# Gated linear attention with a mixture of experts on one core: written order for indirect writes, grouped logits, scan seeds in PSUM, a moved k-v product and early-expert tiles in the first stage's pools

## The chip, the cores and the metric

The kernel runs on 1 core of one Trainium2 chip. A core has TensorE (PE in the profile; PEld is its weight loading), VectorE (DVE), ScalarE (ACT), GpSimd (POOL) and SyncE (SP, which here only issues transfers), each with its own in-order queue of instructions, and 16 DMA engines. The metric is the time of one execution in microseconds on the device. The kernel before has been timed three times; the median is 460.03 us (457.02 to 463.07).

## The reference

First a gated linear attention over 4 batches, 8 heads, 768 tokens and a head dimension of 48, with a 48 x 48 state per head:

```python
for t in range(S):
    state = alpha[:, :, t, :, None] * state + np.einsum('bhd,bhe->bhde', k[:, :, t], v[:, :, t])
    y[:, :, t] = np.einsum('bhd,bhde->bhe', q[:, :, t], state)
```

Its output, 3072 tokens of 384 values, goes through a mixture of 8 experts (384 to 1024 to 384). A token takes the expert with its largest logit, unless a local gate says that it stays with the expert of the token before it:

```python
logits = np.einsum('bsd,de->bse', x, w_gate)
local_gate = 1.0 / (1.0 + np.exp(-np.einsum('bsd,de->bse', x, w_local).squeeze(-1)))
...
        fresh_e = int(np.argmax(logits[b, s]))
        if s == 0 or local_gate[b, s] < 0.5:
            e = fresh_e
        else:
            e = prev_e if prev_e >= 0 else fresh_e
        ...
        h = np.maximum(x[b, s] @ w1[e], 0.0)
        out[b, s] = p[e] * (h @ w2[e])
```

All values are fp32.

## The kernel before, in words

**Attention, 24 blocks.** A block is 128 tokens of one batch, cut into two chunks of 64; the four batches take turns, so block i + 4 continues block i. Four transfers bring `a` (the decays), `k`, `q` and `vt`. Two scans on VectorE, `scan1` forward and `scan2` backward, make products of decays; their second operand is a tile of seeds (`z1`, `z2`), and GpSimd multiplies `q` and `k` with the results in place. `mids` is a small fill by GpSimd of columns of `a`, which `scan1` of that block needs. TensorE then transposes `k` (`kt`, tile kp), multiplies k with q (`pm`, tile pe), k with v (`um`, tile up), and at last forms the output (`ym`, tile y); VectorE masks pe (`mask`), adds the k-v products to the state (`sums`) and carries the state on (`carry`); ScalarE copies states (`first`, tile sb) and results out of PSUM. The block's rows XR go to DRAM (xd), are transposed (`xt`, tile xp), copied to xx, and multiplied with the gate weights (`logit`, tile lg).

The loop at `for i in range(NB + 2)` is a software pipeline over these steps: in pass i, `um`, `sums` and `ym` are those of block i - 1, the scans those of block i + 1, `kt` and `pm` those of block i, and `xt` and `logit` those of block i - 2. Three times in a pass `other()` advances all routing generators by one step each and runs the deferred VectorE work. Four blocks make a column of logits; `logits` and `route` turn columns into an expert number, a probability and a place in that expert's list, for spans of 2, 1, 2 and 1 columns. Each span ends with indirect writes by GpSimd (`ls<-pl,ix` in the profile): one for each block, 8, 4, 8 and 4 of them. In each pass TensorE also does dummy matmuls on the zero tile dz (DN of them, and DN0 = 48 at the start).

**The early expert.** Expert 0's weights come in during the attention stage and are split into a high and a low part (`Weights.split`), and each product is made of three matmuls. Its first 240 tokens (job a) are multiplied in the passes after the last block, its next 240 (job b) after them. `fast` finds job b's tokens for the last span by matmuls without waiting for the list to land.

**The ranked experts.** The other seven are sorted by their token count. For each there is a job with up to four tiles of 128 tokens or fewer: load the list (`li`), gather the tokens (`xg`, an indirect read), transpose and split (`tp`, `xh`, `xl`), first product (`h`, into `hh`, `hl`), second product (`yp`, `yo`), and an indirect write to `out`. The weights of the next expert are loaded and split between the slices of the current one (`piece`): the split's high part on ScalarE, its low part on VectorE or, for one piece (tile w1l), on GpSimd. At last a rarely taken loop treats tokens beyond a list's planned size, whose number is counted in `nt`, `ovt` and `cum`.

**Pools.** Attention's SBUF tiles are in the pool ap, its PSUM tiles in pp (tags kp, up, pe, y, xp, lg, rt; pe takes two banks, so all eight are taken). The early expert's tiles for job a are in m1 and pp. At the end of the `with` block both pools are given up, and the pools mp and qp take their memory; job b's products use mp and qp.

**Order.** A planner orders each engine's instructions by its own estimate of time, except where `keep_in_program_order` holds them to the order of the program; from the first block on that is asked for everything that goes through the `Engine` wrapper (line 80, hence "L80" in every row). `apart` declares that an indirect write does not depend on the earlier ones of its kind:

```python
for p in those:
    tc.declare_no_dep(w.ins, p, reason="every token has a place of its own")
those.append(w.ins)
```

## Time and profile before

| | |
|---|---|
| median of 3 runs | 460.03 us (457.02 to 463.07) |
| the profiled execution, its own time | 461.34 us |
| its span, first to last instruction | 459.5 us |
| mean granted TensorE clock | 0.956 |
| busy: PE, PEld, DVE, ACT, POOL | 416.8, 375.8, 258.7, 167.4, 173.3 us |
| moved by DMA | 64.79 MB |

The profile is one execution. Busy times are shares of the span; a busy TensorE isn't one at its peak, since its matmuls overlap and their ends are modelled. The granted clock is given as a share of full speed. "idle before" names what a waiting engine waited for, inferred from semaphores; "issue" means that nothing visible was waited for. In a row of a timeline the numbers are start and length in us, and brackets hold the idle time before it. In the chain of waits each piece is released by the one before it. The last instruction of TensorE ends at 450.8 us.

### The profile page before, as it was taken

The page shows a single profiled execution, that of the slowest core. Times are in us where ns is not written, and L with a number is a line of the kernel's source. Part 1 is how long each engine was busy: PE and PEld are TensorE (multiplying, and loading weights), DVE is VectorE, ACT ScalarE, POOL GpSimd, SP SyncE. Part 2 cuts the span into 40 slices and gives each one's busy share as a digit, 9 for nine tenths or more (in the row PEclk, how much of TensorE's full clock was granted, in tenths as well). Part 3 has the DMA queues.
Part 4 walks back from the last instruction along what each step waited for, and adds up shares of the span by engine and source line. Part 5 has one row for each costly group of instructions (what it writes and reads, how often), then busy time and mean ns, then how long its engine had stood idle before and what let it go on. Part 6 is the DMA issues. An engine that isn't in the chain of part 4 may idle for free.

```text
span 459.5 us, 10789 instructions
## 1 busy us (share of the span) xinstructions
PE 416.8 (91%) x4245; PEld 375.8 (82%) x4245; DVE 258.7 (56%) x436; ACT 167.4 (36%) x366; POOL 173.3 (38%) x233
## 2 busy tenths in 40 slices
PE   7699999949979988882999799999999999999992
PEld 7578878837858877772988698999999999999992
DVE  4878888927966852361455524634446536466420
ACT  1145555423543452200445314414415324363300
POOL 8433334384365512433525023333334114251012
PEclk9799999996998999996899899999999999999997
DMA  8889878784785610123457513533544716445001
GB/s 218 190 242 270 220 219 243 208 174 89 180 155 161 185 60 19 20 52 123 115 178 184 165 47 108 168 108 106 169 121 134 221 37 201 159 129 184 34 11 31
DMA packets 35476, 64.79 MB, mean 141 GB/s; under 512 B 9942, under 2 KB 17879, under 8 KB 35423
## 3 DMA queue, kind: packets, MB, share of 16 engines
q1 hardware_dynamic: 27420, 53.63, 42.1%
q0 software_dynamic: 6272, 10.09, 7.8%
q8 instruction: 34, 0.56, 0.6%
q10 hardware_dynamic: 1730, 0.36, 0.4%
q14 instruction: 20, 0.16, 0.2%
HBM read 54.51 MB, written 10.11 MB: 141 GB/s over the span
## 4 chain that ended last, share of the span: by engine, by line
PE 49%; issue 9%; POOL 5%; DVE 3%; DMA 2%; ACT 1%; POOLq 0%; SPq 0%; ACTq 0%
PE h_r L80 18%; PE yp_r L80 18%; PE y L80 3%; PE lg L80 2%; POOL out L80 2%; PE tp_r L80 1%; PE hp L80 1%; DMA ls<-pl,ix 1%; PE up L80 1%; POOL w1l_r L80 1%; PE yp_a L80 1%; POOL xg_r L80 1%; DMA rw_r<-w 1%; PE yp_b L80 1%; POOL ls L80 1%
## 5 line engine op out<-in xcount | busy, mean ns | idle before, releaser
L80 POOL DMA_INDIRECT out<-yo_r,li_r x25 | 27.2, 1089 | 116.5 <-DVE yo_r L80 112.6
L80 PE MATMUL yp_r<-w2h_r,hh_r 128*128 128x384 f32 (+4 forms) x200 | 69.7, 348 | 0.0
L80 PE MATMUL yp_r<-w2h_r,hl_r 128*128 128x384 f32 (+4 forms) x200 | 68.0, 340 | 0.0
L80 PE MATMUL yp_r<-w2l_r,hh_r 128*128 128x384 f32 (+4 forms) x200 | 67.9, 339 | 0.0
L80 PE MATMUL h_r<-xl_r,w1h_r 128*128 128x384 f32 (+5 forms) x168 | 59.9, 357 | 0.0
L80 PE MATMUL h_r<-xh_r,w1h_r 128*128 128x384 f32 (+5 forms) x168 | 59.8, 356 | 0.0
L80 PE MATMUL h_r<-xh_r,w1l_r 128*128 128x384 f32 (+5 forms) x168 | 59.7, 355 | 0.0
L80 DVE SCALAR_TENSOR_TENSOR hl_r<-h_r,hh_r 128x384 fp32r<-128x384 f32 (+5 forms) x56 | 33.3, 597 | 43.1 <-ACT hh_r L80 42.5
L80 ACT ACTIVATE hh_r<-h_r 128x384 fp32r<-128x384 f32 (+5 forms) x56 | 29.4, 525 | 66.4 <-PE h_r L80 66.2
L80 POOL TENSOR_TENSOR k<-k,sf 112x512 f32<-112x512 f32 x24 | 28.6, 1193 | 46.3 <-issue 39.5
L80 POOL DMA_INDIRECT xg_r<-xd,li_r x25 | 28.7, 1148 | 38.7 <-DMA li_r<-ls 28.9
L80 DVE TENSOR_TENSOR_SCAN A<-a,z 112x520 f32<-112x520 f32 x24 | 29.6, 1232 | 20.1 <-POOL a L80 20.1
L80 POOL TENSOR_TENSOR q<-q,A 112x512 f32<-112x512 f32 x24 | 28.4, 1183 | 31.3 <-DVE A L80 26.1
L80 PEld LDWEIGHTS yp_r<-w2h_r,hh_r 128*128 128x128 f32 (+4 forms) x200 | 36.7, 183 | 0.3
L80 PEld LDWEIGHTS yp_r<-w2l_r,hh_r 128*128 128x128 f32 (+4 forms) x200 | 36.6, 183 | 0.3
L80 PEld LDWEIGHTS yp_r<-w2h_r,hl_r 128*128 128x128 f32 (+4 forms) x200 | 36.5, 183 | 0.3
L80 DVE TENSOR_TENSOR w2l_r<-rw_r,w2h_r 128x768 fp32r<-128x768 f32 x28 | 34.5, 1232 | 2.9 <-ACT w2h_r L80 1.2
L80 DVE TENSOR_TENSOR_SCAN sf<-a,z 112x520 f32<-112x520 f32 x24 | 34.7, 1445 | 0.1
L80 PE MATMUL y<-sb,q 112*64 112x96 f32 x384 | 29.6, 264 | 4.3 <-ACT sb L80 4.1
L80 PEld LDWEIGHTS h_r<-xl_r,w1h_r 128*128 128x128 f32 x168 | 31.6, 188 | 2.2 <-DVE xl_r L80 0.3
L80 PEld LDWEIGHTS h_r<-xh_r,w1l_r 128*128 128x128 f32 x168 | 31.6, 188 | 2.0
L80 PEld LDWEIGHTS h_r<-xh_r,w1h_r 128*128 128x128 f32 x168 | 31.5, 188 | 2.0
(190 smaller groups left out, 793.7 us busy)
## 6 DMA issues: line engine op xcount, KB each, us to landing
rw_r<-w SPq DMA_DIRECT2D x21, 512.0 KB, 3.9
rw_r<-w SPq DMA_DIRECT2D x28, 384.0 KB, 3.5
a<-akq SPq DMA_DIRECT2D x24, 227.9 KB, 5.2
k<-akq SPq DMA_DIRECT2D x24, 224.0 KB, 4.2
q<-akq SPq DMA_DIRECT2D x24, 224.0 KB, 4.3
vt<-vn SPq DMA_DIRECT2D x24, 192.0 KB, 3.8
xd<-XR SPq DMA_DIRECT2D x24, 192.0 KB, 2.8
vt<-vn SPq DMA_DIRECT2D x24, 96.0 KB, 4.2
```

Of the source, the lines that this page charges most:

```text
L80: r = f(*a, **k)
```

## The change

- `order` adds, for each engine, an edge from every instruction to the one written before it. It is called in the wrapper and, for indirect writes, again in `apart`, after the declarations.
- `DN` falls from 4 to 2, and the dummies move from `logit` to the end of `pm`, into unused columns of pe.
- `logit` does nothing for three blocks and then the matmuls of four blocks, with the gate weights' slice as the outer loop; the blocks write partitions 0, 32, 64 and 96 of a tile in tag rt. The copy lc follows at once, and `logits` has one step less. xx is one tile for four blocks.
- The tag lg goes. Its bank holds `zp`, and `z1` becomes its first 260 columns; `scan1` runs in two halves of 260 over the same seeds.
- `um(i)` moves from the start of the next pass to the end of the pass, ahead of the last `other()`; `sums` and `first(i - 1, 1)` move to the start of the pass, ahead of `scan1(i + 1)`.
- `fast` runs the deferred work first.
- Job b keeps the pools m1 and pp, with job a's tags (xp, up, y, pe and kp); pp is given up only after job b, and the first ranked job transposes its tokens into xp.
- The overflow count's VectorE part moves into the first product of the first ranked job, its matmuls into the fourth slice of the second product.

```diff
-DN = 4
+DN = 2
...
-    pinned = [False]
+    pinned, behind, before = [False], {}, {}
+
+    def order(r):
+        e = r.ins.engine
+        p = behind.get(e)
+        if p == r.ins.name:
+            p = before[e]
+        if p is not None:
+            tc.add_manual_dep(r.ins, p, mybir.DependencyInfo(
+                mybir.DependencyClass.NoSync, mybir.DependencyReason.DATA), reason="written order")
+        behind[e], before[e] = r.ins.name, p
...
-                return tc.keep_in_program_order(r) if pinned[0] else r
+                if pinned[0]:
+                    tc.keep_in_program_order(r)
+                    order(r)
+                return r
...
             tc.declare_no_dep(w.ins, p, reason="every token has a place of its own")
+        order(w)
         those.append(w.ins)
...
-        z1 = ap.tile([R, SW], F32, bufs=1, name="z1")
+        HW = SW // 2
+        zp = pp.tile([128, 512], F32, tag="z", name="zp")
+        z1 = zp[0:R, 0:HW]
...
-            v_.tensor_tensor_scan(A, d["a"][:, 0:SW], z1, 0.0, ALU.mult, ALU.add)
+            for h in range(2):
+                w = slice(h * HW, (h + 1) * HW)
+                v_.tensor_tensor_scan(A[:, w], d["a"][:, w], z1, 0.0, ALU.mult, ALU.add)
...
+            for _ in range(DN):
+                t_.matmul(pe[:, 1, 256:496], lhsT=dz[:, 0:128], rhs=dz[:, 0:240], start=True, stop=True)
             d["pe"] = pe
...
         def logit(i):
-            c, o = i // G, i % G
-            xx = blk[i]["xx"]
-            if o == 0:
-                st["lg"] = pp.tile([128, 368], F32, tag="lg", name=f"lg_{c}")
-            lg = st["lg"]
+            c = i // G
+            if i % G < G - 1:
+                return
+            xx = st["xx"]
+            lg = pp.tile([128, 128], F32, tag="rt", name=f"lg_{c}")
             for k in range(3):
-                t_.matmul(lg[32 * o:32 * (o + 1), 0:128], lhsT=wgs[:, k, :], rhs=xx[:, k, :], start=(k == 0), stop=(k == 2))
-            for _ in range(DN if i + 2 < NB else 0):
-                t_.matmul(lg[:, 128:368], lhsT=dz[:, 0:128], rhs=dz[:, 0:240], start=True, stop=True)
...
+                for b in range(G):
+                    t_.matmul(lg[32 * b:32 * (b + 1), :], lhsT=wgs[:, k, :], rhs=xx[:, b, k, :],
+                              start=(k == 0), stop=(k == 2))
+            lc = ap.tile([128, 128], F32, tag="lc", bufs=1, name=f"lc_{c}")
+            s_.copy(lc, lg)
+            steps.append(logits(c, lc))
...
-            lp = [pp.tile([P, 3], F32, tag=t, name=f"lp_{t}") for t in ("rt", "lg")[0:ns]]
+            lp = [pp.tile([P, 3], F32, tag=t, name=f"lp_{t}") for t in ("rt", "kp")[0:ns]]
...
-        jb = Job("b", PART2, FIRST * RS + C1, m1, None, 2, 2, 9, 4, ("tp", 2), (("yp",), 3))
+        jb = Job("b", PART2, FIRST * RS + C1, m1, pp, 2, 1, 8, 2, ("xp", 1), (("up", "y"), 1))
...
             if 0 < i <= NB:
-                um(i - 1)
+                sums(i - 1)
+                first(i - 1, 1)
             if i + 1 < NB:
                 scan1(i + 1)
             if i < NB:
                 state0(i)
                 kt(i)
-            if 0 < i <= NB:
-                sums(i - 1)
-                first(i - 1, 1)
-            if i < NB:
                 pm(i)
...
             if i > 1:
                 logit(i - 2)
+            if i < NB:
+                um(i)
             other()
...
-    for j in jobs:
-        j.sp, j.ps = mp, qp
+    for j in jobs[1:]:
+        j.sp, j.ps = mp, pp
+    jobs[1].tpt = ("xp", 1)
...
+            if n == 1 and f == 4:
+                nt = mp.tile([8, 1], F32, bufs=1, name="nt")
+                gr = mp.tile([8, NOV], F32, bufs=1, name="gr")
+                v_.tensor_tensor(gr, cntp.broadcast_to([8, NOV]), cc("jt", 0, 8), ALU.is_gt)
+                v_.tensor_reduce(nt, gr, AX.X, ALU.add)
...
         for q, _ in enumerate(j.gemm2(W)):
+            if n == 1 and q == 3:
+                tp = qp.tile([8, 2], F32, tag="tp", name="ovt")
+                t_.matmul(tp[:, 0:1], lhsT=cc("tri8", 0, 8), rhs=nt, start=True, stop=True)
...
+        if n == 0:
+            pc.close()
+            qp = ctx.enter_context(tc.tile_pool(name="qp", bufs=2, space=PSUM))
+            for m in jobs[1:]:
+                m.ps, m.tpt = qp, ("tp", 2)
```

More of the change, by code (lines that the diff above doesn't have):

```diff
@@ L241, in store @@
                 bounds_check=NTOK - 1, oob_is_err=False))
-    with ExitStack() as ac:
+    ac, pc = ExitStack(), ExitStack()
+    pp = pc.enter_context(tc.tile_pool(name="pp", bufs=1, space=PSUM))
+    with ac:
         ap = ac.enter_context(tc.tile_pool(name="ap", bufs=2))
-        pp = ac.enter_context(tc.tile_pool(name="pp", bufs=1, space=PSUM))
         BW = HP * 128
         SW = 2 * HP * (C + 1)
-        z1 = ap.tile([R, SW], F32, bufs=1, name="z1")
+        HW = SW // 2
+        zp = pp.tile([128, 512], F32, tag="z", name="zp")
+        z1 = zp[0:R, 0:HW]
         z2 = ap.tile([128, SW], F32, bufs=1, name="z2")
@@ L805, in gla_moe @@
                     piece(Wn, (f - 3) // 2)
-        if n == 1:
-            nt = mp.tile([8, 1], F32, bufs=1, name="nt")
-            gr = mp.tile([8, NOV], F32, bufs=1, name="gr")
-            v_.tensor_tensor(gr, cntp.broadcast_to([8, NOV]), cc("jt", 0, 8), ALU.is_gt)
-            v_.tensor_reduce(nt, gr, AX.X, ALU.add)
-            tp = qp.tile([8, 2], F32, tag="tp", name="ovt")
-            t_.matmul(tp[:, 0:1], lhsT=cc("tri8", 0, 8), rhs=nt, start=True, stop=True)
-            t_.matmul(tp[:, 1:2], lhsT=cc("ones", 0, 8)[:, 0:8], rhs=nt, start=True, stop=True)
-            cum = mp.tile([8, 2], F32, bufs=1, name="cum")
-            v_.tensor_copy(cum, tp)
-            ti = mp.tile([8, 1], I32, bufs=1, name="ti")
-            v_.tensor_copy(ti, cum[:, 1:2])
         at_ = spread(nx.ns, 4 * j.ns) if nx else []
@@ L820, in gla_moe @@
         for q, _ in enumerate(j.gemm2(W)):
+            if n == 1 and q == 3:
+                tp = qp.tile([8, 2], F32, tag="tp", name="ovt")
+                t_.matmul(tp[:, 0:1], lhsT=cc("tri8", 0, 8), rhs=nt, start=True, stop=True)
+                t_.matmul(tp[:, 1:2], lhsT=cc("ones", 0, 8)[:, 0:8], rhs=nt, start=True, stop=True)
+                cum = mp.tile([8, 2], F32, bufs=1, name="cum")
+                v_.tensor_copy(cum, tp)
+                ti = mp.tile([8, 1], I32, bufs=1, name="ti")
+                v_.tensor_copy(ti, cum[:, 1:2])
             if nx and q in (0, 2):
```

36 lines of the change are left out of this document (17 added, 19 removed).

## The prediction

> **What bounds the kernel now.** I read the table by stretches first, with the stretches cut where TensorE changes its behaviour. The first row is one line of the answer on the tile XR, the copy that ends each block's attention.
>
> ```profile
> L80 ACT COPY XR<-y x24: 478/478/479, 21.0 to 182.8; 128x384 f32<-128x384 f32 x24
> ...
> 26.80:95.90 69.10, 68.04 (x1256) 55.24 (x1255) 58.62 (x92) 36.95 (x98) 28.25 (x37) 1.00 0.83 235
> 95.90:111.10 15.20, 9.10 (x115) 7.42 (x116) 6.66 (x14) 3.22 (x10) 9.73 (x13) 0.69 0.58 100
> 111.10:182.80 71.70, 66.26 (x1140) 53.92 (x1140) 47.08 (x89) 32.76 (x92) 30.02 (x35) 0.97 0.52 129
> ...
> 205.60:216.30 10.70, 1.23 (x9) 0.85 (x9) 1.86 (x8) 0.82 (x2) 4.81 (x5) 0.75 0.49 155
> 216.30:237.40 21.10, 20.71 (x133) 19.86 (x133) 10.71 (x19) 8.86 (x17) 7.52 (x6) 0.88 0.49 142
> ...
> 254.30:257.10 2.80, 0.04 (x1) 0.01 (x1) 1.90 (x4) 2.72 (x4) 0.00 (x0) 1.00 0.38 152
> 257.10:262.10 5.00, 4.98 (x23) 4.97 (x24) 2.59 (x4) 0.49 (x1) 0.00 (x0) 0.66 0.72 181
> 262.10:450.80 188.70, 188.70 (x1078) 183.88 (x1076) 91.67 (x125) 64.58 (x106) 56.99 (x46) 1.00 0.39 120
> 450.80:459.50 8.70, 0.00 (x1) 0.00 (x0) 0.62 (x1) 0.00 (x0) 1.32 (x1) 0.64 0.15 34
> ```
>
> The columns are the stretch and its length, busy time of PE, PEld, DVE, ACT and POOL, the granted clock, the DMA share and GB/s. Three kinds of stretch stand out. In 262 to 451 us TensorE is busy all of the time at clock 1.00, and the change leaves that work alone, as it does the 8.70 us behind it. In the attention stage (24 copies of XR from 21.0 to 182.8, so 23 block periods in 161.8 us, 7.03 us each) it is nearly always busy, except in 95.9 to 111.1. And there are two holes: 205.6 to 216.3 (1.23 of 10.70 us busy) and 254.3 to 257.1 (0.04 of 2.80). After each hole the clock is low for a while (0.88 and 0.66 over the next stretch), so a hole costs more than its length.
>
> One undisturbed block, from the chain of waits (start, length, what), and inside it the logits from the timeline of PE:
>
> ```profile
> 151.01 2.21 PE y L80 x48
> 153.22 1.42 PE lg L80 x10
> 154.63 0.81 PE up L80 x16
> 155.44 0.53 PE kp L80 x4
> 155.98 0.62 PE pe L80 x32
> 156.60 0.48 PE xp L80 x3
> ```
> ```profile
> 153.15 0.84 PE L80 MATMUL lg<-xx,wgs 128*32 128x128 f32 x6
> 153.92 0.71 PE L80 MATMUL lg<-dz 128*128 128x240 f32 x4
> 154.56 0.88 PE L80 MATMUL up<-vt,kk 128*48 128x96 f32 x16
> ```
>
> A block is 2.21 + 1.42 + 0.81 + 0.53 + 0.62 + 0.48 = 6.07 us of PE with nothing idle in between. 23 of them would be 139.6 us, so 22.2 us of the 161.8 are excess.
>
> **The change part by part.**
>
> *Written order for indirect writes.* This is what the planner made of group 0's eight list writes on POOL (first and last of eight), and what DVE and POOL did next:
>
> ```profile
> 91.28 1.43 POOL L80 DMA_INDIRECT ls<-pl,ix  x1 [1.50 <-DVE st L80]
> ...
> 100.86 0.98 POOL L80 DMA_INDIRECT ls<-pl,ix  x1 [0.30 <-issue]
> 101.85 1.19 POOL L80 TENSOR_TENSOR q<-q,A 112x512 f32<-112x512 f32 x1
> ...
> 105.61 1.18 POOL L80 TENSOR_TENSOR q<-q,A 112x512 f32<-112x512 f32 x1 [1.41 <-DVE A L80]
> 108.02 1.18 POOL L80 TENSOR_TENSOR k<-k,sf 112x512 f32<-112x512 f32 x1 [1.23 <-issue]
> ```
> ```profile
> 104.24 1.24 DVE L80 TENSOR_TENSOR_SCAN A<-a,z 112x520 f32<-112x520 f32 x1 [8.97 <-POOL a L80]
> 105.51 0.18 DVE L80 RECIPROCAL z<-A 112x4 f32<-112x4 f32 x1
> 105.61 0.53 DVE L80 TENSOR_TENSOR st<-up,st 112x384 f32<-112x384 f32 x1
> 106.05 1.83 DVE L80 TENSOR_TENSOR_SCAN sf<-a,z 112x520 f32<-112x520 f32 x1
> ```
>
> All eight stand in a row in front of one block's q product, so POOL gives nothing to the blocks for 10.6 us and the scan waits 8.97 us. The 15.20 us stretch holds one block: 15.2 - 6.07 = 9.1 us lost, partly as low clock (0.69). In written order at most two writes fall in one pass of the block loop, one after the k product and one after the small fill of "a" that the next scan needs. A write is (100.86 + 0.98 - 91.28) / 8 = 1.32 us on POOL. The one ahead of the fill makes the next scan late, the one behind it runs beside that scan. Group 0 and 1 have 12 writes and the early expert 2 gathers, 7 passes. I charge 1.0 us each, 7 us (bounds 0, where TensorE is the limit, and 7 x 1.32 = 9).
>
> *Dummies and logits.* Four dummies go from 153.92 to 154.56, 0.64 us; two stand in their place behind pe, 0.32 to 0.42 with the same edges, I take 0.40. The six real logit instructions take 0.77 us (153.15 to 153.92), 0.13 each, one behind the other. In the new form 24 stand together and neighbours write different column groups. Rows of this kind: up, two groups, 0.81 / 16 = 0.05 each at 96 columns, 0.067 at 128; pe, four quadrants, 0.62 / 32 = 0.02 at 64 columns. So 24 cost 0.9 us (four abreast, as pe) to 1.6 (two, as up) to 3.1 (no overlap), per block 0.23, 0.40, 0.77. I take 0.30; no gain below pe's price is in sight. PE per block becomes 6.07 - 1.42 + 0.40 + 0.30 = 5.35 us.
>
> *k-v product at the block's end, state sum ahead of the scan.* On PE "um" only changes places with its neighbours. On DVE it adds a wait: the state sum of block i-1, which needs that product, now stands ahead of scan 1 of block i+1, and behind it queue the scan, POOL's q, scan 2, POOL's k, and PE's transposes of k. From the rows above: scan at 104.24 to the end of k at 108.02 + 1.18 = 109.20 is 4.96 us, with the second scan stretched from 1.23 to 1.83 because q still runs on POOL. With the sum in front: 0.53 + 4.96 = 5.49 us from the end of one um to the start of the k transposes two blocks on. The PE work of that block follows, 5.35 us, and ends with its um. So two periods take at least 5.49 + 5.35.
>
> *Scan seeds in PSUM, in two halves.* The elements stay the same, one instruction more. A small DVE instruction is 0.18 us (the reciprocal), so between 0 and 0.36 is added; I take 0.15, since two instructions overlap at their edges as 105.51 and 105.61 do. Two periods: 5.49 + 0.15 + 5.35 = 11.0, a period of 5.5 us. That is above the 5.35 of PE: the loop over DVE and POOL becomes the limit by a little.
>
> ```profile
> L80 DVE TENSOR_TENSOR_SCAN A<-a,z x24: 1222/1228/1242, 4.7 to 158.8; 112x520 f32<-112x520 f32 x24
> ...
> 66.45 1.21 DVE L80 TENSOR_TENSOR w1l_a<-rw_a,w1h_a 128x1024 fp32r<-128x1024 f32 x1
> ```
>
> The minimum, median and maximum of the scan are the same, so nothing on POOL ever held it up, and moving its seeds buys nothing against today's neighbours. It matters for the write that will run beside it: the scan's wait for such a write would be up to 0.98 us in 7 passes, 3.5 us over pairs of passes, which my sum leaves out. The Trainium skill, "SBUF — State Buffer", section "SBUF: two separate sides", says that DVE with two SBUF inputs and GpSimd take one port pair in turns for a whole instruction; the stretched sf row agrees, and by that rule the scan with a PSUM operand is free of the lock, so leaving the 3.5 us out is right.
>
> In 13 blocks the early expert's weight splits (7 pieces, every second pass) stand between the two scans: 1.21 us for the row shown. Beside q they aren't free, I add 1.0: two periods 12.0, so 6.0 us. The attention stage: 13 x 6.0 + 10 x 5.5 = 133, + 7 for writes, + 5 (estimate: of today's 71.7 - 10 x 6.07 = 11 us of excess in 111.1 to 182.8 about half is routing work and the early expert's matmuls, which stay) = 145 us against 161.8. **Gain 17.**
>
> *One step less in the routing.* The logits' copy is no longer a step of its own; at the end each step is a slice of the early expert's matmuls, about 1 us. **Gain 1.**
>
> *Early expert on own buffers.* The hole, and what follows it up to the first ranked expert:
>
> ```profile
> 207.52 0.81 PE L80 MATMUL tp_b<-cs,xg_b 120*128 120x120 f32 x6 [0.35 <-PE ct L80]
> 216.26 0.54 PE L80 MATMUL h_b<-xh_b,w1h_a 128*128 128x240 f32 x1 [7.93 <-ACT xh_b L80]
> ...
> 215.34 0.82 ACT L80 CAST xh_b<-tp_b 128x360 fp32r<-128x360 f32 x2 [18.95 <-DMA out<-yo_a,li_a]
> ```
> ```profile
> 215.24 1.79 DMA li_r<-ls
> ...
> 220.62 1.00 POOL xg_r L80
> ...
> 224.51 2.41 POOL w1l_r L80
> 226.94 3.57 DMA rw_r<-w
> 230.54 1.06 ACT w1h_r L80
> ...
> 237.40 16.96 PE h_r L80 x72
> ```
>
> The cast has its input at 208.3 and waits until 215.3, for DMAs that have nothing to do with it: its tile lies in memory of a pool that must first be given up. With tiles of job a's pools that wait goes. One transposed tile at a time (one buffer) costs two rounds of transposes 0.4, cast 0.4 and difference 0.5: matmuls at about 210.0 instead of 216.26. Part b and the first transposes take 21.10 us at clock 0.88; at 1.00 that is 18.6, so PE could end at 228.6 instead of 237.4. What is late next: the list load ends at 217.0, three gathers at 1.3 each (ahead of the weight difference on POOL) bring 221.9, the difference 2.41, the load into its buffer 3.57, the cast 1.06: 229.0, and one more cast and difference until about 231. PE starts at 228.6 but waits inside its first group, as if it began at 230.7. **Gain 6.7** (9 if those weights come in time, 4 if the pool that is now given up between part b and the first ranked expert costs a wait).
>
> *Overflow count earlier.*
>
> ```profile
> 257.12 0.23 PE L80 MATMUL ovt<-nt,cs 8*8 8x1 f32 x4 [2.77 <-DVE nt L80]
> ```
>
> The count moves to the fourth slice, its matmuls into the second product: 2.77 us go, and 5.0 x (1 - 0.66) = 1.7 of low clock behind it. **Gain 4** of the 4.5, as some of it may meet weights that come no earlier.
>
> **Sum.** 17 + 1 + 6.7 + 4 = 29 against the profiled execution's 461.3 (span 459.5): 433. That execution is 1.3 us above the median of the runs, so **432 us**.
>
> **The rivals.** *TensorE stays the limit.* The new DVE wait is hidden and writes cost nothing: 23 x 5.35 + 5 = 128, a gain of 34, with the full 9 and 4.5: 417 us. For it: PE is the limit in every undisturbed block today. Against: the loop above is 5.5.
>
> *The loop keeps its old pace.* DVE is busy 58.62 of 69.10 us and the DMA share is 0.83 in 26.8 to 95.9. If that holds blocks at 6.07 us: 139.6 + 7 + 5 = 152, a gain of 10, and 4 + 3 elsewhere: 443 us.
>
> *The order does not spread the writes.* Then the 9.1 us stay and the 7 are saved, with a shorter burst of group 1 adding some 5: about 439.
>
> *The clock falls (slower).* Half the dummies go, and PE gets short pauses. In the row 257.1 to 262.1 a pause of 2.77 us was enough for 0.66. A block at half clock costs about 5 us more (5.35 doubled, less what overlaps); the gain of 29 is gone with 6 such blocks, and with 12 the time is 432 + 60 = 490. Against it: 111.1 to 182.8 has PE busy for 92% and a clock of 0.97, and my blocks of 6.0 us have PE busy for 89%. The Trainium skill, "TensorE: Matmul & The Clock Gate", section "Why this matters for your kernels", asks for no idle gaps above about 3 us; the trace is stricter, with 2.77 us.
>
> **How the numbers follow.** Forecast 0.55 (424 to 440), TensorE as the limit 0.18, old pace 0.16, not spread 0.05, clock 0.06. The range 416 to 447 leaves out the clock and small parts of the others. About 2% (451 us) is what can be told from no change; all cases but the clock lie below it, and I move some chance to the middle for small costs that add up: faster 0.87, same 0.07, slower 0.06.
>
> **What would show it.** Periods of XR: 5.4 to 5.6 without and 6.0 with splits; list writes one or two per block; lg in groups of 24 within 0.9 to 1.6 us; no wait of xh_b for a DMA; h_b 2 to 2.5 us behind tp_b; ovt without a wait. The forecast is wrong if the scan waits for the state sum longer than the 0.5 us, if a clock under 0.9 stands in the attention stage, or if the first ranked expert's matmuls still begin more than 27 us behind tp_b (29.9 today, 237.40 - 207.52; 23 by my sum).

## The result and the profile after

The changed kernel takes 455.54 us (median of 20 runs, 452.45 to 458.73) against 459.53 us for the kernel before (20 runs, 457.02 to 464.48): a ratio of 0.990, 95% interval 0.988 to 0.993. That is 4 us less, where 28 were forecast; the forecast range was 416 to 447 us.

Below are the line of the tile XR of the kernel after, and its table by stretches, cut at the same events as before (columns as there):

```profile
L90 ACT COPY XR<-y x24: 474/478/482, 21.3 to 178.6; 128x384 f32<-128x384 f32 x24
```
```profile
21.20:95.50 74.30, 62.26 (x1245) 52.19 (x1247) 69.43 (x104) 36.65 (x97) 32.08 (x37) 0.90 0.77 215
95.50:132.00 36.50, 28.03 (x581) 23.12 (x579) 33.15 (x59) 17.10 (x49) 24.08 (x26) 0.95 0.87 184
132.00:179.10 47.10, 40.66 (x744) 33.98 (x743) 33.58 (x60) 21.42 (x60) 20.30 (x25) 0.89 0.39 113
179.10:204.40 25.30, 22.35 (x151) 20.38 (x149) 10.34 (x50) 3.58 (x13) 11.49 (x13) 0.87 0.20 54
...
208.50:235.60 27.10, 22.24 (x133) 20.57 (x133) 11.24 (x19) 9.27 (x17) 7.53 (x6) 0.87 0.41 124
235.60:445.40 209.80, 209.75 (x1171) 201.28 (x1171) 105.23 (x144) 75.20 (x121) 66.28 (x52) 1.00 0.42 126
```

TensorE, which was busy for 68.04 of 69.10 us in the first part of the attention stage, is now busy for 62.26 of 74.30, and the clock there is 0.90 instead of 1.00. VectorE, 58.62 of 69.10 before, has become 69.43 of 74.30. The two profiled executions (461.34 and 455.79 us; spans 459.5 and 453.9) differ stage by stage like this:

| stage | before, us | after, us | change | forecast |
|---|---|---|---|---|
| first to last XR | 161.8 | 157.4 | -4.4 | -17 |
| last XR to the first transpose of part b (tp_b) | 24.8 | 27.2 | +2.4 | -1 |
| first tp_b to the first product of the ranked experts (h_r) | 29.7 | 29.8 | 0 | -6.7 |
| first h_r to TensorE's end | 213.6 | 209.8 | -3.8 | -4 |

So one term out of four arrived. The attention stage differs from profile to profile: three runs with the same attention code, below, have 156.7 to 159.5 us from the first XR to the last block's output, with 21 to 34 us of it at half clock, so the comparisons below rest on ratios of many executions and use the stages as a hint. The ratios use fast executions alone, and the profiles of two later runs (e_three_h and e_write_slot) fell on slow ones, so their stages are left out below.

**What sets the pace now.** VectorE's timeline of one undisturbed block after, without a weight split, and GpSimd's of the same block:

```profile
33.59 0.55 DVE L90 COPY st<-up 112x384 f32<-112x384 f32 x1
34.06 1.27 DVE L90 TENSOR_TENSOR_SCAN A<-a,zp 112x260 f32<-112x260 f32 x2
35.36 0.18 DVE L90 RECIPROCAL z<-A 112x4 f32<-112x4 f32 x1
35.58 2.16 DVE L90 TENSOR_TENSOR_SCAN sf<-a,z 112x520 f32<-112x520 f32 x1
37.66 0.66 DVE L90 TENSOR_TENSOR pq<-pe,cs 128x512 f32<-128x512 f32 x1
38.25 1.02 DVE L90 SCALAR_TENSOR_TENSOR st<-st,en 112x192 f32<-112x192 f32 x1
39.19 0.55 DVE L90 TENSOR_TENSOR st<-up,st 112x384 f32<-112x384 f32 x1
```
```profile
35.46 1.18 POOL L90 TENSOR_TENSOR q<-q,A 112x512 f32<-112x512 f32 x1 [1.96 <-DMA k<-akq]
37.87 1.18 POOL L90 TENSOR_TENSOR k<-k,sf 112x512 f32<-112x512 f32 x1 [1.23 <-DMA a<-akq]
```

From one state sum to the next are 39.19 - 33.59 = 5.60 us, and VectorE has no idle time in them. Two of its six instructions are stretched: the second scan takes 2.16 us where 1.23 is its usual time; GpSimd's q product runs until 36.64, and the scan ends 1.10 us later. The carry takes 1.02 us beside the k product; that is its median in the kernel before too, where its shortest is 0.35. The scan's median over the 24 blocks went from 1.23 to 2.16 us. (By the Trainium skill, "SBUF — State Buffer", section "SBUF: two separate sides", whichever of such a pair starts first keeps the shared port pair for its whole instruction; these rows agree.) TensorE's timeline shows who pays, at the same place and later:

```profile
33.51 0.60 PE L90 MATMUL kp<-cs,k 112*128 112x112 f32 x4 [0.94 <-POOL a L90]
...
37.30 0.88 PE L90 MATMUL up<-vt,kk 128*48 128x96 f32 x16
...
58.02 0.60 PE L90 MATMUL kp<-cs,k 112*128 112x112 f32 x4 [1.99 <-POOL a L90]
...
75.23 0.60 PE L90 MATMUL rp<-cs,kr 128*32 128x128 f32 x4 [2.40 <-DVE kr L90]
...
106.26 0.38 PE L90 MATMUL rp<-cs,kr 128*32 128x128 f32 x2 [3.00 <-DVE kr L90]
```

TensorE waits 0.94 us for the k product in every such block (the row names the fill of a, which GpSimd does next), 1.99 us where a weight split stands in front and no logits are due, and 2.40 and 3.00 us where a step of the routing stands on VectorE between the two scans. The k-v product (up) ended at 38.18, and the state sum that reads it began at 39.19: the sum did not wait for TensorE here, VectorE's own row made it late. Over the run the sum waited for its product 8 times, 12.2 us in all (longest 3.3), against 18 times and 23.6 us in the kernel before.

Longer pauses are often followed by half the clock. Here is the stretch behind the pause that ends at 58.0 us:

```profile
59.30:62.70 3.40, 3.40 (x35) 2.85 (x37) 3.33 (x4) 1.86 (x6) 1.50 (x2) 0.50 0.73 177
```

Between the first XR and the last block's output the record of the granted clock has 27.8 us at 0.5 (15.8 before). Of the nine pauses of 1.4 to 3.0 us in this stage six were followed by such a stretch, and three (1.44, 1.75 and 1.96 us) were not.

**Between the stages** the cast xh_b waits for no DMA any more, and part b's first product starts 2.7 us behind the first tp_b (2 to 2.5 forecast). But that product now has three waits for VectorE of its own (0.90, 0.90 and 1.38 us), and its clock is low. The lines are the cast from ScalarE's timeline, the product's start and the first of the three waits from TensorE's, and two of the last links of the chain of waits up to h_r:

```profile
206.37 0.46 ACT L90 CAST xh_b<-tp_b 128x360 fp32r<-128x360 f32 x1 [16.19 <-PE tp_b L90]
```
```profile
208.53 0.38 PE L90 MATMUL hp<-xh_b,w1h_a 128*128 128x240 f32 x1 [0.55 <-ACT xh_b L90]
...
211.72 0.57 PE L90 MATMUL hp<-xh_b,w1h_a 128*128 128x240 f32 x1 [0.90 <-DVE hl_b L90]
```
```profile
222.58 4.78 DMA rw_r<-w
...
235.57 0.47 PE h_r L90
```

The wait of 7.93 us has become several small ones, and a weight load stands in the chain.

**List writes and overflow count** look as forecast. Writes on GpSimd in one pass (of group 0), and the count's matmuls, without a wait:

```profile
94.09 1.18 POOL L90 DMA_INDIRECT ls<-pl,ix  x1 [0.17 <-POOL k L90]
95.26 0.12 POOL L90 MEMSET a<- 112x4 f32 x1
95.56 0.98 POOL L90 DMA_INDIRECT ls<-pl,ix  x1 [0.18 <-issue]
```
```profile
256.79 0.24 PE L90 MATMUL ovt<-nt,cs 8*8 8x1 f32 x4
```

### The profile page after: what moved, and what is told of

Its sections match the earlier page's. It is cut to its first block, busy times and chain, and to the rows that moved or that the text cites. A ratio compares the mean times of both kernels' runs of the same rounds, so it can differ in the third digit from the quotient of the medians.

```text
span 453.9 us, 10713 instructions
## 1 busy us (share of the span) xinstructions
PE 403.4 (89%) x4205; PEld 367.7 (81%) x4205; DVE 276.9 (61%) x460; ACT 167.6 (37%) x366; POOL 180.5 (40%) x233
## 4 chain that ended last, share of the span: by engine, by line
PE 59%; DVE 2%; issue 2%; ACT 2%; DMA 1%; POOL 0%; POOLq 0%; ACTq 0%
PE yp_r L90 22%; PE h_r L90 22%; PE hp L90 3%; PE yp_a L90 2%; PE y L90 2%; PE tp_r L90 2%; DMA rw_r<-w 1%; PE yp_b L90 1%; PE up L90 1%; PE h_b L90 1%; PE h_a L90 0%; PE pe L90 0%; PE lg L90 0%; PE kp L90 0%; PE tp_a L90 0%
## 5 line engine op out<-in xcount | busy, mean ns | idle before, releaser
L90 POOL DMA_INDIRECT out<-yo_r,li_r x25 | 27.2, 1089 | 110.9 <-DVE yo_r L90 98.1
L90 POOL TENSOR_TENSOR q<-q,A 112x512 f32<-112x512 f32 x24 | 36.3, 1512 | 42.6 <-DVE A L90 17.4
L90 ACT COPY sb<-st 48x192 f32<-48x192 f32 x88 | 30.8, 350 | 38.9 <-DVE st L90 37.4
L90 DVE TENSOR_TENSOR_SCAN sf<-a,z 112x520 f32<-112x520 f32 x24 | 44.8, 1868 | 0.4
L90 DVE TENSOR_TENSOR_SCAN A<-a,zp 112x260 f32<-112x260 f32 x48 | 30.5, 676 | 9.3 <-POOL a L90 9.3
```

The costliest lines, as they stand in the source:

```text
L90: r = f(*a, **k)
```

## The experiments

The kernel before took about 460 us in two groups of runs and 468 us in four; each ratio is against the kernel before in its own group, and times expected in us are on the scale of 459.5 us for the kernel before. "Stage" is the time from the first XR to the end of TensorE's output for the last block in the run's profile, "half" what of it the clock was at 0.5, "seam" the first tp_b to the first h_r. Stage, half and seam are of one profiled execution each. The seam of the code before is not one number: e_order_only and e_ovt_only, which have that code and stand in groups of 468 us, show 27.2 and 27.7 us, the profile of the kernel before in its group of 460 us shows 29.7.

| run | ratio to before | 95% interval | stage, us | half, us | seam, us |
|---|---|---|---|---|---|
| before | 1 | | 161.7 | 15.8 | 29.7 |
| after | 0.990 | 0.988 to 0.993 | 157.3 | 27.8 | 29.8 |
| e_after_again | 0.991 | 0.987 to 0.995 | 156.7 | 20.9 | 29.5 |
| e_order_only | 0.982 | 0.974 to 0.990 | 152.2 | 3.0 | 27.2 |
| e_no_order | 1.032 | 1.024 to 1.040 | 176.9 | 65.0 | 32.3 |
| e_ovt_only | 0.993 | 0.991 to 0.996 | 161.3 | 19.5 | 27.7 |
| e_seed_sbuf | 0.992 | 0.988 to 0.996 | 162.7 | 47.1 | 29.8 |
| e_sums_after | 0.969 | 0.963 to 0.975 | 151.1 | 23.8 | 30.0 |
| e_um_front | 0.989 | 0.984 to 0.993 | 160.1 | 47.7 | 30.0 |
| e_um_dn8 | 0.977 | 0.970 to 0.983 | 149.8 | 10.2 | 30.7 |
| e_dn4 | 0.982 | 0.979 to 0.985 | 156.1 | 17.6 | 29.2 |
| e_sums_dn4 | 0.975 | 0.971 to 0.979 | 148.9 | 15.3 | 29.6 |
| e_three_h | 0.990 | 0.986 to 0.994 | | | 30.0 |
| e_seam | 0.983 | 0.976 to 0.990 | 159.5 | 34.4 | 25.5 |
| e_best_a | 0.964 | 0.961 to 0.968 | 151.0 | 19.8 | 25.0 |
| e_best_b | 0.974 | 0.969 to 0.978 | 154.3 | 30.5 | 24.3 |
| e_best_w | 0.953 | 0.949 to 0.957 | 148.7 | 25.4 | 24.6 |
| e_best_bw | 0.965 | 0.962 to 0.969 | 154.9 | 35.0 | 25.7 |
| e_best_y | 0.947 | 0.944 to 0.951 | 144.7 | 18.4 | 24.3 |
| e_write_slot | 0.988 | 0.982 to 0.994 | | | |

My theory after the result was: the state sum ahead of the scan takes away VectorE's lead over TensorE, so that everything on VectorE stops TensorE, and these pauses halve the clock; and between the stages TensorE's work and the weights are late by the same amount. The rivals were: fewer dummies alone let the clock fall; the written order itself costs, since routing products on TensorE come too early; halves of the scan cost.

### The anchor

The changed kernel as it is.

> The changed kernel once more, on a chip where the kernel before takes about 468 us instead of 459.5. It anchors the other ratios. If the chip slows both kernels alike: 0.988 to 0.993 of the kernel before, as at first. If the chip's slowness sits in something that the change touches, the ratio moves.

Measured 0.991. The ratio holds in a group where the kernel before takes 468 us, so ratios of different groups can be compared.

### Written order, alone and taken out

```diff
 (e_order_only: to the kernel before)          (e_no_order: to the changed kernel)
+                    order(r)                  -                    order(r)
...
+        order(w)                              -        order(w)
```

> The kernel before plus the written order for indirect writes, nothing else. By the prediction's terms: the row of eight list writes goes (9.1 us), up to 7 us come back spread over 7 blocks where TensorE doesn't hide them; with VectorE 2 to 3 us ahead of TensorE, as in the kernel before, most of the 1.3 us writes are hidden: 450 to 455 us. If the order itself costs (TensorE waits on routing tiles, as the changed kernel shows): 457 to 462.

> The changed kernel without the written order (the planner places the indirect writes). If the order is worth something in the changed kernel: list writes stand in rows of seven and three again, one block is stretched by about 9 us, and the time is 457 to 464. If the order only moves the loss from one block to many: 452 to 457, no difference that can be told.

Order alone gives 0.982, some 8.3 us (4.8 to 12 by its interval): about the 9.1 us of the burst, with little or nothing paid back. GpSimd's timeline of that run shows a write between the q and the k product instead of eight in a row, and the table by stretches shows TensorE busy for 144.40 of 152.30 us at clock 0.99:

```profile
92.45 1.56 POOL L90 TENSOR_TENSOR q<-q,A 112x512 f32<-112x512 f32 x1
94.17 1.76 POOL L90 DMA_INDIRECT ls<-pl,ix  x1 [0.16 <-issue]
95.96 1.19 POOL L90 TENSOR_TENSOR k<-k,sf 112x512 f32<-112x512 f32 x1
```
```profile
20.90:173.20 152.30, 144.40 (x2610) 117.74 (x2611) 123.79 (x200) 75.22 (x205) 76.75 (x87) 0.99 0.71 184
```

Without it the changed kernel is slower than the kernel before by 3.2% (474 us on the scale of the expectation, which ended at 464). The same row of writes (first and last of eight) costs more here, and the clock in the stretch around it is 0.67.

```profile
94.73 1.18 POOL L90 DMA_INDIRECT ls<-pl,ix  x1 [1.54 <-DVE ix L90]
...
104.47 0.97 POOL L90 DMA_INDIRECT ls<-pl,ix  x1 [0.30 <-issue]
```
```profile
89.00:130.00 41.00, 28.72 (x452) 23.85 (x453) 25.77 (x53) 14.08 (x39) 20.20 (x22) 0.67 0.57 128
```

So the rival that the order itself costs falls.

### The overflow count alone

```diff
 (to the kernel before)
+            if n == 1 and f == 4:
+                nt = mp.tile([8, 1], F32, bufs=1, name="nt")
...
+            if n == 1 and q == 3:
+                tp = qp.tile([8, 2], F32, tag="tp", name="ovt")
```

> The kernel before with one edit: the overflow count's VectorE part at the fourth slice of the first ranked expert and its small products in the second product. By the prediction's term 2.77 us of waiting and 1.7 us of low clock go: 4 us, 0.988 to 0.994 of the kernel before. If weights that come no earlier take the gain back: 0.995 to 1.0.

The ratio is 0.993, that is 3.1 us (1.9 to 4.4 by its interval); from the first h_r to TensorE's end are 209.1 us instead of 213.6. The term of 4 us holds.

### Seeds back in SBUF

```diff
-        HW = SW // 2
-        zp = pp.tile([128, 512], F32, tag="z", name="zp")
-        z1 = zp[0:R, 0:HW]
+        HW = SW
+        z1 = ap.tile([R, SW], F32, bufs=1, name="z1")
...
-            for h in range(2):
+            for h in range(1):
```

> The changed kernel with the scan's seeds in SBUF and one scan of 520 elements, as in the kernel before, all else as changed. The prediction charged 0.15 us per pair of periods for the two halves and left out a wait of the scan for list writes. If seeds in PSUM are worth nothing: periods of 5.55 to 5.6 us and the time within 3 us of the changed kernel (0.985 to 0.997 of the kernel before). If a scan with SBUF operands is held up by GpSimd's work beside it: scans of 1.8 us and more where a write or a product runs, the period above 5.7, and 0.995 to 1.01.

The ratio is 0.992 against 0.990 and 0.991: no difference that can be told. The scan's line on its tile, of this run and of the kernel after:

```profile
L90 DVE TENSOR_TENSOR_SCAN A<-a,z x24: 1224/1231/1243, 5.0 to 163.7; 112x520 f32<-112x520 f32 x24
```
```profile
L90 DVE TENSOR_TENSOR_SCAN A<-a,zp x48: 661/674/696, 5.0 to 157.9; 112x260 f32<-112x260 f32 x48
```

Neither form was ever held up (maximum 1243 ns for one scan, 696 for a half), although list writes run beside it: in e_seed_sbuf one scan overlaps a write for 1.10 us and takes 1.24. The halves cost 1.27 - 1.23 = 0.04 us; the 0.15 charged was too much, and the 3.5 us left out exist in neither form.

### Where the state sum stands

```diff
 (e_sums_after: to the changed kernel)
-            if 0 < i <= NB:
-                sums(i - 1)
-                first(i - 1, 1)
             if i + 1 < NB:
                 scan1(i + 1)
             if i < NB:
                 state0(i)
                 kt(i)
+            if 0 < i <= NB:
+                sums(i - 1)
+                first(i - 1, 1)
+            if i < NB:
                 pm(i)
 (e_um_front: this, and um back at the pass's start)
+            if 0 < i <= NB:
+                um(i - 1)
             if i + 1 < NB:
                 scan1(i + 1)
...
-            if i < NB:
-                um(i)
```

> The changed kernel with one part moved back: the state sum of block i-1 and its first carry stand behind scan 1 and the k transposes of the next block again, as in the kernel before; the k-v product stays at the pass's end, everything else as changed. Theory L (the sum ahead of the scan ties VectorE to TensorE's last product, so VectorE has no lead, and routing steps and weight splits stop TensorE): VectorE runs ahead again, XR periods 5.4 to 5.6 in undisturbed blocks and under 7 in the blocks that cost 10 now, the attention stage (first to last XR) 140 to 148 us instead of 157.4, the time 440 to 447. Rival C (two dummies instead of four let the clock fall, and the low clock makes the long blocks): the blocks of about 10 us stay with their half-clock stretches, the time 452 to 456. Rival R (the routing's TensorE steps come too early in written order): the waits of 2.4 to 3.0 us ahead of rp and pw stay, 448 to 453.

> The changed kernel with the whole move of the k-v product undone: product at the pass's start, state sum and first carry behind scan 1 and the k transposes, as in the kernel before; the rest as changed. Without the moved sum alone the changed kernel came to 0.969 of the kernel before. If only the sum's place ahead of the scan cost: 0.965 to 0.975, no matter where the product stands. If the product at the block's end is itself worth something (the sum finds its input ready): 0.975 to 0.99, with waits of VectorE for the product.

Moving the sum alone back gives 0.969 (445 us on the scale of the expectation): 10 us less than the change by the ratios, 6.2 us in the stage by the two profiles. VectorE's timeline of this run, in a pass with a weight split:

```profile
51.94 1.27 DVE L90 TENSOR_TENSOR_SCAN A<-a,zp 112x260 f32<-112x260 f32 x2
...
54.08 0.56 DVE L90 TENSOR_TENSOR st<-up,st 112x384 f32<-112x384 f32 x1 [0.66 <-PE up L90]
54.74 1.23 DVE L90 TENSOR_TENSOR w1l_a<-rw_a,w1h_a 128x1024 fp32r<-128x1024 f32 x1
55.88 1.23 DVE L90 TENSOR_TENSOR_SCAN sf<-a,z 112x520 f32<-112x520 f32 x1
```

The sum stands between the scans again, the second scan meets less of the q product and takes 1.23 us (median of the run 1.23), and VectorE has idle time. Undisturbed periods of XR are 4.7 to 5.5 us (5.4 to 5.6 expected). But the stage took 151.1 us, not 140 to 148, and its half-clock time fell only from 27.8 to 23.8 us. (The 34 us of the next expectations count a stretch behind the stage as well.) The waits ahead of rp fell from 2.40 and 3.00 us to 0.75 and 1.03, so these products don't stand too early as such. So the sum's place explains half or more of the 12.6 us missing in the stage, not all.

With um back as well the gain is gone (0.989, near the end of the second range of the expectation): the product at the block's end is worth 2% as long as the sum doesn't go ahead of the scan. This run has the short second scan too (median 1.23 us), so the scan's stretch alone doesn't decide the time. Its profile has 47.7 us at half clock, and a pause of 3.35 us at 39.8 us for a load that comes late; e_sums_after has that pause too (2.76 us), the changed kernel, whose blocks are slower there, doesn't.

### Dummies and the clock

```diff
-DN = 2
+DN = 4       (e_dn4: to the changed kernel; e_sums_dn4: to e_sums_after)
+DN = 8       (e_um_dn8: to e_um_front)
```

> The changed kernel with four dummy products per block again instead of two, all else as changed. Theory L (the loop over VectorE and GpSimd is the limit): the two more dummies, about 0.3 us, go where TensorE waits 0.94 us per block for the k transposes only if they stand in front of that wait; they stand right behind the scores, so the undisturbed period stays 5.6 us or grows to 5.9, and half-clock stretches behind pauses of 2 us and more stay: 0.985 to 1.005 of the kernel before. Rival C (fewer dummies let the clock fall): half-clock stretches in the attention stage fall from about 34 us to 17 or less and the time to 0.96 to 0.98 of the kernel before.

> Both edits: the state sum behind scan 1 again, and four dummies per block. Without the second edit this was 0.969 of the kernel before, with undisturbed periods of 4.7 to 5.5 us and about 34 us at half clock in the attention stage. Theory L: TensorE is near its limit, so 0.3 us more per block is paid in undisturbed blocks (+3 to +7 us), unless input loads set the pace there; 0.97 to 0.985. Rival C: the half-clock stretches shrink by more than that costs: 0.945 to 0.965.

> The changed kernel with the move of the k-v product undone, as in the run that came to 0.989 of the kernel before with 48 us at half clock in the attention stage, and with eight dummy products per block instead of two (some 0.65 us more TensorE work per block, 15 us in all). Theory K (TensorE is faster than its suppliers, so it pauses, and pauses of 1.4 us and more bring the half clock, which costs more than the work saved): pauses and half-clock stretches shrink to under 20 us and the time falls to 0.965 to 0.982 in spite of more work. Rival (the low clock only goes with waits that would be there anyway): the time stays or grows with the work, 0.99 to 1.01.

Two more dummies in the changed kernel gave 0.982 (0.985 by the median of all its ten executions), a gain of 0.5 to 0.9%, between the two ranges of the expectation; in its profile the stage is hardly shorter (156.1 us, 17.6 at half clock). In e_sums_after they gave nothing (intervals overlap), as the first theory of that expectation has it. The third run has the largest dose. Here is e_um_front's stage in two parts, and then e_um_dn8's:

```profile
21.30:98.90 77.60, 70.13 (x1324) 58.09 (x1328) 65.09 (x109) 39.59 (x105) 31.14 (x40) 0.87 0.78 212
98.90:181.40 82.50, 71.74 (x1234) 59.60 (x1230) 55.48 (x112) 36.30 (x101) 39.80 (x48) 0.83 0.55 140
```
```profile
19.70:92.70 73.00, 69.18 (x1396) 59.19 (x1398) 70.36 (x110) 39.22 (x104) 34.44 (x42) 1.00 0.84 229
92.70:169.50 76.80, 70.59 (x1295) 59.57 (x1294) 58.53 (x113) 36.33 (x101) 41.53 (x48) 0.93 0.60 149
```

Six more dummies per block make the kernel faster by 1.2% (0.989 to 0.977; the intervals just miss each other), the clock goes from 0.85 to 0.96, and half-clock time from 47.7 to 10.2 us. More work on TensorE made the kernel faster, so the rival of the dummies holds a part beside my theory. But this run does not show that the clock alone did it: with eight dummies the early blocks take 5.2 us instead of 4.7, the late load of e_um_front is in time, and its pause of 3.35 us and the 10.2 us at half clock behind it are gone as well. What such a pause is worth by itself is seen below in e_best_w (1%).

What goes with the low clock can be estimated from three runs with the same attention code (after, e_after_again, e_seam): stage 157.3, 156.7, 159.5 us with 27.8, 20.9, 34.4 us at half clock. That is (159.5 - 156.7) / (34.4 - 20.9), about 0.2 us for each us at half clock. The clock recorded with every execution gives the same size: over the 20 executions of the changed kernel the half-clock time of the whole span, 2 x (1 - clock) x span, goes from 46 to 70 us, and the time rises by 0.16 us for each us of it (correlation 0.59). Pauses lengthen both, so the part that the clock itself causes may be less. For e_um_front the estimate is 37.5 x 0.2 = 8 us of the 10.3 by which e_um_dn8's stage is shorter; but these two profiles lie at the far ends of their runs (465.71 us where the median is 461.59, and 445.99 where it is 448.03), and by the ratios the difference is 5.5 us.

It also bears on the account of the change. Order and overflow count alone come to 0.982 x 0.993 = 0.975. The change with the whole move of um undone, which is these two with fewer dummies, grouped logits, PSUM seeds and the own buffers, is at 0.989: these parts together cost 1.4% there instead of saving, and dummies give most of it back. Some 2 to 3 us of that stand in the seam (30.0 against 27.2 and 27.7 us), and the late load is another piece; the parts were not taken out one by one.

### Between the stages

```diff
 (e_three_h)
-        ja.h, jb.h = halves(ja), halves(jb)
+        def thirds(j):
+            def h(f):
+                return pp.tile([128, j.n], F32, tag=("kp", "rt", "z")[f % 3], name=f"h_{j.nm}_{f}")
+            return h
+        ja.h, jb.h = halves(ja), thirds(jb)
 (e_seam: this, and)
-                if f in (3, 5, 7):
+                if n == 0 and f in (0, 2, 4):
+                    piece(Wn, f // 2)
+                if n and f in (3, 5, 7):
                     piece(Wn, (f - 3) // 2)
```

> The changed kernel with one edit: part b's hidden products go to three tiles of their own in turn instead of two banks of one tile and a third tile. Theory T (one tile over two banks makes the matmuls into one bank wait for VectorE's read of the other): the three pauses of 0.9 to 1.4 us in part b's first product go, that product takes 9 to 12 us instead of 15.7, the first ranked expert starts 3 to 6 us earlier, and the time is 449 to 453. Rival W (the ranked expert's weights are as late as its TensorE work): the gain ends at 1 us or less, 454 to 456, with a new wait of h_r for its weights.

> The changed kernel with two edits between the stages: part b's hidden products in three tiles of their own, and the first ranked expert's three first weight pieces split at slices 0, 2 and 4 of part b instead of 3, 5 and 7. The three tiles alone gave nothing. Theory W (TensorE's work and the weights are late by about the same amount, so that either alone gives nothing): both together start the first ranked expert 3 to 6 us earlier, 0.978 to 0.985 of the kernel before. Rival: the weight loads themselves (five loads queued behind buffers) set the time, less than 1 us, 0.988 to 0.993.

With three tiles the waits of 0.90 to 1.38 us are gone, and h_r starts 30.0 us behind tp_b instead of 29.8. The chain of waits shows what took their place: the products wait for transposes, these for a weight split and a load.

```profile
233.23 0.88 DVE w2l_r L90
...
234.13 3.70 DMA rw_r<-w
...
238.42 0.90 PE tp_r L90 x3
...
247.31 0.71 PE h_r L90 x2
```

With the first weight pieces earlier as well, the seam is 25.5 us (24.3 to 25.7 in all runs that have both edits), 4.3 less, and the ratio 0.983, whose interval still touches that of the changed kernel. Mending the products alone gives nothing. That fits products and weights that are late by about the same amount, but the weights alone were not tried, so it is not shown that both edits are needed.

### Versions that beat both kernels

```diff
 (e_best_a: e_sums_after and e_seam together; e_best_w: e_best_a and)
-            if w == -2:
-                EW.load()
+            if w == -2 or w == 1:
                 EW.load()
 (e_best_b: e_best_a and; e_best_bw: both)
-            s_.copy(d["end"], end)
+            s_.mul(d["end"], end, 1.0 / SEED)
...
-                v_.scalar_tensor_tensor(sn[:, 0], d["s3"][:, 2], 1.0 / SEED, d["end"].unsqueeze(2).broadcast_to([R, HP, D]),
-                                        ALU.mult, ALU.mult)
+                g_.tensor_tensor(sn[:, 0], d["s3"][:, 2], d["end"].unsqueeze(2).broadcast_to([R, HP, D]), ALU.mult)
 (e_best_y: e_best_w and; e_write_slot: to the changed kernel)
                 v_.tensor_copy(cF, ps[:, :, n])
             yield
+            if cb < NBB:
+                yield
```

> Both places mended together: the state sum behind scan 1, and the two edits between the stages (three tiles for part b's hidden products, first weight pieces earlier). If the two are independent, the product of both ratios: 0.969 and the 3 to 6 us of the edits between the stages give 0.956 to 0.963 of the kernel before. If the second gives nothing: 0.967 to 0.972.

> The best version so far (state sum behind scan 1, three tiles for part b, earlier first weight pieces; 0.964 of the kernel before) with one more edit: the carry of the state to the block four later goes from VectorE (1.03 us per block, stretched by GpSimd's k product beside it) to GpSimd, as a plain product. Theory V (VectorE is now the limit: 11.0 us of work in two passes, one of them with a weight split, so 5.5 us per block): periods of 4.7 to 5.0 us instead of 5.3 to 5.5 in undisturbed blocks, 4 to 10 us less, 0.944 to 0.956. Rival D (input loads set the pace): pauses and periods stay, 0.962 to 0.968; worse if GpSimd's longer row makes the scans late.

> The best version so far with one of the early expert's first two weight loads (0.5 MB) moved from the third pass to the sixth, where the second split doesn't need it yet. Theory D (the scan's input of the seventh block comes late behind 1 MB of weights): the pause of 3.4 us near 40 us and the half-clock stretch behind it go or shrink, 3 to 6 us less, 0.951 to 0.958. If the late input only moves to another block: 0.962 to 0.968.

> Both edits, the carry on GpSimd and the later weight load. If both causes hold and add: 0.93 to 0.948 of the kernel before. If only one holds, the better of the two single ones.

> The version with 0.953 of the kernel before (state sum behind scan 1, both edits between the stages, later weight load), with one more edit: one more step of the routing's schedule ahead of the list writes, so that one write stands behind the fill of a that the next scan needs and the other between the q and the k product, where GpSimd waits for the second scan anyway. If the write ahead of the fill costs what VectorE waits there (1.1 to 1.3 us in seven passes, partly hidden): 3 to 7 us less, 0.938 to 0.947. If TensorE or other waits cover it: 0.951 to 0.956.

> The changed kernel with this one edit: list writes one step later, none ahead of the fill of a. The prediction's term for the writes was 7 us, 1.0 us in each of seven passes. If they cost that in the changed kernel: 0.976 to 0.984 of the kernel before. If the scan waits there for the state sum in front of it anyway: 0.988 to 0.994.

e_best_a, 0.964: the two edits add, within the noise, since 0.969 x 0.983 / 0.990 is 0.962.

e_best_w, 0.953: moving one of the early expert's weight loads to a later pass is worth 1%. GpSimd's timeline of e_best_a shows the fill of "a" waiting 3.20 us for its load, and TensorE's shows the pause that follows, which is 0.97 us in e_best_w:

```profile
39.39 0.11 POOL L90 MEMSET a<- 112x4 f32 x1 [3.20 <-DMA a<-akq]
```
```profile
43.00 1.23 PE L90 MATMUL y<-sb,q 112*64 112x96 f32 x12 [3.38 <-ACT sb L90]
```

e_best_b and e_best_bw, 0.974 and 0.965: taking the carry off VectorE made each 1% slower, where the expectation had named this only as a risk; undisturbed periods stayed at 5.5 us. The trace of e_best_b shows what sets them there: the carry now stands on GpSimd ahead of the fill of a, and scan 1 waits for that fill 19 times, 29.7 us in all (4 times and 5.9 us in e_best_a). From VectorE's timeline of e_best_b:

```profile
50.27 1.28 DVE L90 TENSOR_TENSOR_SCAN A<-a,zp 112x260 f32<-112x260 f32 x2 [1.23 <-POOL a L90]
```

What sets 5.3 to 5.5 us in e_best_a wasn't found.

e_best_y, 0.947 (444.05 us where the kernel before took 468.55; e_best_w 439.23 where it took 461.25): the intervals of e_best_y and e_best_w overlap by little, so the moved writes are worth 0 to 1.3%. In the changed kernel itself (e_write_slot, 0.988) they make no difference that can be told, as expected if the scan waits there for the sum. Stage 144.7 and seam 24.3 us of e_best_y are near what the prediction had forecast for the change (145 and 23), but with five edits more:

```profile
21.20:165.90 144.70, 130.17 (x2556) 108.40 (x2554) 126.43 (x220) 74.82 (x205) 74.19 (x87) 0.94 0.73 194
...
200.00:223.90 23.90, 20.76 (x137) 19.58 (x136) 11.79 (x20) 9.91 (x19) 9.50 (x8) 0.93 0.50 155
```

Not tried: the fill of "a" ahead of the writes instead, or on VectorE.

## Why the prediction was wrong

*What bounds the kernel, and the pace.* This is the step that failed, in the attention stage: 17 us were forecast and 4.4 came. "The loop over DVE and POOL becomes the limit by a little", 5.5 us, came out as 5.60 us in undisturbed blocks, and as 6.13 in the mean where every second pass has a weight split (5.60 and 6.65; 6.0 forecast). The size was right by luck, since the sum was the wrong one. I priced "it adds a wait" of VectorE for the k-v product, in a chain of two periods, and never added up VectorE's own row: 0.55 + 1.27 + 0.18 + 2.16 + 0.66 + 1.02 = 5.84 us, 5.60 with the overlapping edges. The wait is rarer than before (8 sums against 18), the row is what fills the period, and an engine whose row fills the period has no lead. So the mis-sized term is what interrupts the blocks: 13 x 6.13 + 10 x 5.60 = 135.7 us (133 forecast), and the stage took 157.4. The other 21.7 us, for which 7 + 5 stood in the sum, go with routing steps and writes that now stop TensorE, and with the half clock behind these pauses: by 0.2 us per us, 27.8 us of it are some 6 (an estimate). How the rest divides was not measured.

*Written order.* The 9.1 us and where they come from were right (e_order_only 8.3 us); the 7 us charged for the spread were too much: little or nothing in the kernel before, no difference that can be told in the changed kernel, at most 1.3% in the best version.

*Dummies and logits.* The prices were right or too high: 24 logit products take 0.86 us (0.9 to 3.1 in the bounds), two dummies 0.33 us from their start to that of the next matmul (0.40 taken). A TensorE block came to 4.7 us in e_sums_after, and to 4.9 with a quarter of the 0.86; 5.35 were forecast. But less work on TensorE brought nothing by itself, as TensorE wasn't the limit any more.

*The rival with TensorE as the limit* was mis-added: 460 - 34 - 9 - 4.5 is about 412, not 417 us. It did not come about.

*The clock rival,* 0.06, came half true: its mechanism is seen, its price of 5 us for a cold block and its point of 6 cold blocks were too coarse. I took 111.1 to 182.8 before, busy for 92% at clock 0.97, as evidence against it. But that kernel had no pause above 1.4 us there, and the changed one has nine of 1.4 to 3.0 us in its stage. A pause of 1.99 us was enough at 56 us, and so it was in e_after_again; e_seam, with the same attention code, has one of 1.98 us there, and its clock stays at 1.00 until 76 us. So the length of a pause alone doesn't decide. The Trainium skill, "TensorE: Matmul & The Clock Gate", section "Why this matters for your kernels", asks for no idle gaps above about 3 us; here pauses of 1.41 to 1.99 us were followed by half clock in some cases.

*Early expert on own buffers.* This is the second step that failed: 6.7 us were forecast and 0 came. The cast's wait went as forecast, with the first product 2.7 us behind tp_b (2 to 2.5 forecast). "At 1.00 that is 18.6, so PE could end at 228.6" failed: the first product has three waits of 0.9 to 1.4 us, and 6.8 us of low clock stand in it. All of part b's hidden products go to one tile over two banks and one more; with three tiles (e_three_h) these waits are gone. TensorE came to h_r at 235.57. The weights, "until about 231", were late too: e_three_h then waits for them, and only with earlier weights the seam falls to 25.5 us.

*One step less in the routing* (1 us) was not seen: the stretch from the last XR to tp_b grew by 2.4 us, with the clock at 0.87 in it (1.00 before).

*Overflow count,* 4 us forecast: 3.8 measured. *Scan seeds:* nothing gained, as said, and they cost 0.04 us per block instead of 0.15 per pair of blocks.

The conditions named for a wrong forecast were the right ones: the clock is 0.89 in the last part of the stage, h_r began 29.8 us behind tp_b, more than 27, and where the sum had to wait it waited for up to 3.3 us.

## What to carry to other kernels

Before pricing a chain of waits, add up each engine's own row over one period, with instructions at the length they have beside their neighbours; an engine that fills the period passes every extra step straight on. Work taken off an engine that then isn't the limit is no gain, and on TensorE it can be a loss: here some 0.7 us of dummy products per block made one version 1.2% faster, with less time at half clock and with a late load in time again. Where two causes may be late by the same amount, mending one may show nothing; look at both before dropping either.

## What the runs showed of the hardware

Pauses of 1.4 to 3.4 us on TensorE were often, but not always, followed by stretches at half clock of 3.4 to 13.7 us (in the changed kernel's stage six of nine pauses, 3.4 or 6.8 us). With each us at half clock went about 0.2 us of this kernel's time (0.16 over 20 executions).

In the runs of the four groups where the kernel before takes 468 us, ScalarE's copy of the last block's rows starts 5.7 to 8.4 us after TensorE's last product for it has ended by the records; in the others 0.05 us (the kernel before itself was profiled in a group of 460 us only). From ScalarE's and TensorE's timelines of e_after_again:

```profile
184.96 0.48 ACT L90 COPY XR<-y 128x384 f32<-128x384 f32 x1 [9.74 <-remote]
```
```profile
175.56 1.13 PE L90 MATMUL y<-vt,pq 64*64 64x48 f32 x32
```

The last product ends at 176.69, the copy starts at 184.96. It goes with the 8 us between 460 and 468, and it hits e_ovt_only too, whose attention stage is that of the kernel before. Its cause stays open.
